# Float32 scores for the first 256 tokens only, in a hashed-attention and Mish feed-forward kernel

## The chip, the cores and the metric

The kernel runs on one core of one Trainium2 chip. The metric is the device time of one execution in microseconds (us): the median of several runs. A profile is one more execution, recorded instruction by instruction by the hardware profiler.

The engines are named as in the profile: PE is the matrix engine (PEld its weight loads), DVE the vector engine, ACT the scalar engine, POOL the GpSimd engine, and SP the queue from which all DMAs of this kernel are issued.

## The reference, cut to what matters

```python
# q, k, v: (4 batches, 8 heads, 768 tokens, 64), float32; proj: (64, 6)
q_bucket = sum((q @ proj > 0) * 2 ** arange(6));  k_bucket = the same of k
scores = where(q_bucket == k_bucket, q @ k.T / 8, -1e9)
attn   = exp(scores - max);  attn /= sum(attn) + 1e-9
x      = (attn @ v), heads side by side          # 3072 tokens x 512
h      = x @ w_in                                # 512 -> 2048
out    = (h * tanh(softplus(h))) @ w_out         # 2048 -> 512; w_in, w_out arrive as float64
```

## The kernel before, in words

The work is cut into **units** of 256 tokens: three units make one of the four batches, twelve units in all (u = 0 to 11). A unit has eight **slots** of attention, one for each of its two halves of 128 tokens and each of four pairs of heads (pair j = 0 to 3); slot n belongs to unit n // 8. A slot S computes 128 x 768 scores for both heads of its pair; then the row maxima (line 978, DVE), the factors of the softmax ("mb", lines 961 to 973), two exponentials (line 991, ACT), and the division with a split into two fp16 halves (lines 387 to 416) follow. The halves are transposed by DMA (line 472, tile PT) and multiplied with V (line 1088). In unit 0 alone the attention weights stay float32 and are transposed on PE (line 434), the product with V is float32 (line 1062), and so are its two feed-forward products (lines 1120 and 1169). The feed-forward part of a unit (H, Mish, O) runs three blocks of four slots behind its attention, and the sixteen pieces of the two float64 weights are converted on ACT, DVE and POOL during units 0 and 1 (lines 594 to 607, and w_hi and w_lo).

**Two ways to compute scores.** The usual way holds Q and K as two fp16 halves side by side in the contraction, and hash bits as six signs beside a second copy: a slot is eight fp16 matmuls (`pe` in att_front, line 937). To get there a block of keys or queries is squared and summed (line 480), scaled into a high half (k_hi, q_hi), copied (k_cp, q_cp), reduced to the low half (k_lo, q_lo), transposed by DMA, hashed by small matmuls (line 739), reduced (hsum, line 743), turned into bits (line 748) and transposed by DMA once more. The halves are laid out in the two buffers tok0 and tok1 before their transposes; units' queries and these keys share them, so one preparation follows the other.

The other way, `pe32` (line 948), takes raw float32 Q and K, transposed on PE (`turn32`, line 450, copied out at line 453), and bits from a float32 hash matmul (`hash32`, lines 461 and 464). It needs no fp16 preparation. F32U says how many units use it, and NF how many pairs: in the kernel before, F32U = 3 and NF = 2, so in units 0, 1 and 2 (the whole first batch) pairs 0 and 1 use float32 scores and pairs 2 and 3 the fp16 ones. The keys of these two pairs are transposed once, at the start (`k_prep32`); the queries of units 1 and 2 once for each unit (`q_prep32`), and their other eight heads go the fp16 way (`q_prep` from column 8 on, by `q_cuts`).

**The order.** The functions only list operations. ORDER, a table found offline, names them by number in the order in which they are issued to the engines; every engine takes its own in that order. A letter behind a number picks an alternative engine from the operation's list (none is the first of them).

Of the kernel before, what the change touches and what calls it, by code (L numbers as in the profile page):

```python
# [93 lines left out]
137 7 9 8 50 20 0 5 11 19 12 22 1 2 3 4 76 80 29 81b 13 37 6 77b 14 15 10 25 33 26 30b 38 17 27 28 18 34 39 52  # L94
60 61 35 62 41 56 54 63 57 55 21 42 48 51 53 24 23 31 78 36 32 64 65 16 86 91 138 92 79 87 147 40 88 82 117 83
43 118 44 119b 93 89 66 109 110 111 153 90 94 120 67 112 154b 132 107d 46 108 133 113 95 115 68 114 116 124
125b 155 121 126 101 84 45 134 136 135 156 127b 178 96 128 140b 148 141 47 58 149 85 122d 123 97 99 142 139b
98b 143 129 168d 179 180d 100 174 176 69 175 177 170 130 157 171b 131 172 173b 204 205b 169 70 145b 182 189
144b 102 158 159 181 161b 190b 71 193 291 194 195 185 191 150 186 192 220 221 103 222d 183b 187 206 160b 196
188 197 104 223 212 152 146 49 151 162 59 105 106 213b 207 216 218 217b 219b 214 215b 184 353 224 243 163 239  # L100
164 244 245b 241 248 240 242 233c 270 368 307 210d 208 235 254 236 255 249 209b 237 246 238 247 225 256 271
250 257 234 272d 262 263 268 266 292 198 273 226 267b 211 227 293 165 294 269 251 283 284 349 350 264 303 265
285 295 166 304b 354 305 296 258 199 200 309d 286b 310 311c 260c 261 306 274 281 313 253 252 232 228 282 312b
322 201 317 364 287 365 288 289 290 366 318 319 355b 323 324 308 320 321 367 330b 331 315 338 339 72 231 203
202 167 229 397 369b 314 329 316 325 297 298b 275 276b 340 333 341 230 332b 334 342 73 370d 299 336 425c 277
74 426 371 399 378 379 380 335 328 302 400 398 300 373 424 423 351 337 301 280 381 427 372b 374 382 389c 411
376 259 375 278 279 406 429 458 428 390 412 452 407 352 391 383 384b 393 392c 395 326 327 385 453 408d 409 410
415d 343 344c 356c 416 451 430 456 345 431 432 394 377 459 386 418 346 457 396 401 417b 454 433 387 348 347
413 419 455 75 357 434 443d 488b 460 421 444 461 420 388 422 441 404 435 436 414 402 445 489 490b 447 437 462d
463 464 478d 403 446c 449 479 405 465 438 466b 471 472b 487 523 518 493 494 495c 486 358 359 467 496 480b 482b  # L110
497 448 481b 484 360 491 510 525 532 511 442 450 361 512b 533 534 535 362 526 524 468 483 513b 492 439 546 514
474 536 552 485 469 470 537 519b 475c 476 516 473 520 538c 539 553 515 517 586 540b 521 554 440 477 498 499b
500 501 555d 542 522 541c 556 557 573b 574 575 548 549b 550 527 503 502 544 577 590 545 543 578 528 530 504
505b 591 592 547 588 506 594 593 507 576b 595d 587 581 612 603 604 551 582 583b 579 596 598c 529 559 558 531
589 597 613 599 580 363 618 600 560 561 562 614d 616 584b 615 632c 563 564c 601 566 651 508 509 585 633 647
634c 648 655 659 640 617 567 649 636 650 652 664 653 605 635 656 565 619 620 621 660 654 638 622 623c 625 568
569 602 639 661d 609 668 606 641 663 662 681b 682 683c 642 626 637 570b 691 607b 608 685 657 665 666 571b 627
# [12 lines left out]
964 952 962 965b 938 986 967 953 981 980 995c 974c 1029 1067 1031 983 987 1005 1004 996 997c 999b 975b 988  # L130
998b 1001b 1006 1007b 1009 1008 966 1066 1010 1011 1012b 990 1158 1021 870 886 1032 1192 1193 984b 993 991 992
994 1022 1023 1019 1003 1033 1069 1030 1194 1024 1000 1014 1025 1039d 1050 1002 1015 1223 1068 985 1013c 1040
1016b 1017 1051 1052d 1041c 1070 1071c 1053 1043 1054 1195 1055c 1042b 1034 1044 1073 1018 1082 1077 1020 1038
1196 989 1045 1083 1074 1086 1056 1057b 1059 1058c 1061b 1072b 1046 1060 1063 1078 1079c 1081 1080 1095c 1197
1064b 1096 1105 1106 1107c 1108 1097b 1098b 1198 1084 1099 1109 1087 1110b 1111 1062 1112 1101b 1036 1047
1085b 1090 1100 1102 1121 1122 1035 1123 1114 1124 1150 1154 1125 1075c 1076 1113b 1127c 1128 1116 1088b 1129b
1093 1155 1136 1137 1138 1104 1168 1119 1037 1115 1117 1139 1131 1140 1048 1091 1130c 1133 1141b 1142 1143b
1145 1151 1159 1089 1160 1132 1144 1161 1103 1164 1118 1120 1134 1146 1147 1162 1163 1152b 1199 1177d 1156
1178 1092 1200 1179b 1181b 1094 1187 1126 1065 1148 1172 1049 1201 1188 1189c 1165 1190 1191 1207c 1252 1182
1218 1180c 1183 1157 1184 1208 1209c 1153 1166 1211b 1224 1169 1175 1173 1225 1219 1220d 1221 1222 1174 1176  # L140
1210c 1213 1253 1212 1135 1149 1185 1170b 1236c 1237 1239 1238 1226 1228b 1214 1229 1186 1215 1247 1282 1202
1278 1216 1248 1249 1250 1203 1240 1251 1267c 1242 1167b 1268 1205b 1269c 1171 1271 1286 1287 1288b 1241 1283
1279 1230 1235 1243 1204b 1206 1280b 1295 1291 1284 1290 1289 1270c 1273 1285 1405 1308d 1281b 1309 1231 1310c
1272 1227 1254 1255 1274 1318 1256 1275 1257 1258c 1233b 1319 1232 1260 1320 1312 1311b 1314 1234 1299 1217
1292 1321 1322 1313 1338 1339 1340c 1304c 1349 1244 1350 1302 1300 1296 1401 1301 1351b 1342b 1261 1315 1293b
1276 1397 1341b 1305 1406 1297c 1353 1294 1303 1344 1352 1245 1355d 1356 1364 1317 1262 1316 1402 1259 1398
1418 1357c 1365 1324 1462 1343 1323 1345 1359 1263 1366 1367 1368 1265 1264b 1298b 1409 1360 1347 1388c 1389
1325 1326 1358b 1361 1399c 1327 1414 1346 1410 1411 1390 1391 1412 1392 1413 1394 1328 1306b 1307b 1403 1266
1329b 1431 1432 1400 1246 1362 1433c 1441 1442 1330c 1443 1393 1395 1331 1415 1419 1354 1348 1396 1435 1444
1434 1445 1370 1369 1332 1422 1457 1363 1425 1423 1416c 1437 1446d 1404 1447 1448b 1450b 1424 1426 1371 1372  # L150
1458 1459d 1333 1334 1336 1461 1460 1475c 1439 1373 1440 1454 1486 1502 1436 1438 1503 1374 1375 1335 1420
1384 1377 1449c 1476 1452 1451 1478c 1407 1487 1488b 1477b 1479b 1489 1490 1337 1506 1378 1379 1380 1453 1480
1515 1510 1421b 1376b 1504 1505b 1381b 1382b 1417 1481 1482 1491b 1507 1492 1493c 1495 1511 1494 1463 1464
1465c 1467 1408 1496 1512d 1383 1807 1516 1513 1514 1528d 1455 1456 1497 1529 1474 1385 1386 1519 1538 1520
1539 1540c 1499 1587 1517b 1530b 1532b 1541 1387 1468 1469 1483 1498 1542 1543c 1544 1545 1484 1470 1531b
1518b 1534 1591 1466c 1427c 1521 1522 1554 1641 1277 1500 1642 1523 1588 1547b 1555 1643 1556 1533 1535 1537
1536 1583 1508b 1557 1558 1509 1428 1584 1524 1569 1471b 1546b 1472b 1548 1473 1429c 1560b 1561 1570 1571c
# [62 lines left out]
F32U = 3  # L220
# [1125 lines left out]
```

## Time and profile before

| | |
|---|---|
| median of 3 runs | 817.49 us (816.95 to 817.76) |
| the profiled execution | 817.2 us, of which the profile's span is 815.4 us |
| busy time in the span | PE 798.2, ACT 624.9, DVE 602.9, POOL 426.9 us |
| first slots of units 0, 1, 2, 3 start at | 14.9, 56.0, 120.5, 198.4 us |

Busy time is the union of an engine's instructions; a wait inside the span is idle time. Views by stretch give the same for a window of the span. In the timeline, a line is a run of like instructions with its start and its duration; the difference between the starts of two neighbouring lines is the time that the first one took from the engine.

### The profile page before, as it was taken

What the parts mean: (1) busy time and instruction counts of PE and PEld (TensorE: products, weight loads), DVE (VectorE), ACT (ScalarE), POOL (GpSimd) and SP (SyncE); (2) the same over time, 40 slices, a digit from 0 to 9 for tenths busy, and PEclk for the clock granted to TensorE, in tenths of its full rate; (3) what the DMA queues carried; (4) which work ended last, traced back from release to release, by engine and by line L of the source; (5) the groups of instructions that cost most, each with busy time, mean ns of one, the idle gap of its engine ahead of it and who ended that gap; (6) DMA issues with size and microseconds to landing.
All of it is one profiled execution on the core that took longest, in us unless ns stands there. A gap on an engine that the chain in (4) does not pass through costs nothing.

```text
span 815.4 us, 17000 instructions
## 1 busy us (share of the span) xinstructions
PE 798.2 (98%) x6546; PEld 549.6 (67%) x6546; DVE 602.9 (74%) x1103; ACT 624.9 (77%) x976; POOL 426.9 (52%) x434
## 2 busy tenths in 40 slices
PE   8899999999999999999999999999999999999998
PEld 5556666666676776676666676667676676776674
DVE  5888999988898778887887767768877675566211
ACT  4889998888696769889679698989779785677211
POOL 3564446554356773733585564344646758845120
PEclk9999999999999999999999999999999999999999
DMA  7958998989999969989989959999989577466200
GB/s 253 219 174 221 240 246 196 191 156 206 217 160 182 203 116 181 170 158 216 185 172 155 195 117 151 197 213 192 167 140 169 107 139 145 81 124 133 50 27 27
DMA packets 395489, 134.29 MB, mean 165 GB/s; under 512 B 365456, under 2 KB 386448, under 8 KB 395408
## 3 DMA queue, kind: packets, MB, share of 16 engines
q1 hardware_dynamic: 395408, 133.21, 81.2%
q8 instruction: 51, 0.84, 0.4%
q14 instruction: 30, 0.25, 0.1%
HBM read 35.65 MB, written 6.29 MB: 51 GB/s over the span
## 4 chain that ended last, share of the span: by engine, by line
PE 47%; ACT 1%; DVE 1%; DMA 1%; issue 0%; POOL 0%; SPq 0%; ACTq 0%; DVEq 0%
PE ps_s L937 7%; PE ps_o L1179 6%; PE ps_o L1181 6%; PE ps_o L1180 6%; PE ps_acc L1130 5%; PE ps_t L1088 5%; PE ps_acc L1132 5%; PE ps_acc L1131 5%; ACT pb L991 1%; DVE svb L978 1%; DMA out_dram<-ffb 1%; PE ps_t L739 0%; ACT L1315 0%; DVE hl L408 0%; ACT tok L480 0%
## 5 line engine op out<-in xcount | busy, mean ns | idle before, releaser
L991 ACT ACTIVATE pb<-ps_s,svb 128x768 f32<-128x768 f32 x184 | 180.9, 987 | 87.4 <-DVE svb L968 36.7
L978 DVE TENSOR_REDUCE svb<-ps_s 128x2 f32<-128x1536 f32 x92 | 161.3, 1753 | 40.2 <-PE ps_s L937 33.7
L1130 PE MATMUL ps_acc<-X,wo 128*128 128x256 f16 x616 | 167.9, 273 | 0.3 <-ACT ffb L1151 0.3
L1132 PE MATMUL ps_acc<-X,wo 128*128 128x256 f16 x616 | 167.9, 273 | 0.0
L1131 PE MATMUL ps_acc<-X,wo 128*128 128x256 f16 x616 | 167.9, 273 | 0.0
L1315 ACT ACT_TABLE_LOAD x117 | 150.1, 1283 | 2.0
L408 DVE SCALAR_TENSOR_TENSOR hl<-pb,svb,hl 128x768 f16<-128x768 f32 x131 | 140.3, 1078 | 13.8 <-POOL hl L390 9.8
L1181 PE MATMUL ps_o<-wi,ffb 128*128 128x512 f16 x352 | 133.4, 379 | 0.0
L1180 PE MATMUL ps_o<-wi,ffb 128*128 128x512 f16 x352 | 133.4, 379 | 0.0
L1179 PE MATMUL ps_o<-wi,ffb 128*128 128x512 f16 x352 | 133.4, 379 | 0.0
L937 PE MATMUL ps_s<-KT,QT 128*128 128x512 f16 (+1 forms) x656 | 120.1, 326 | 2.1 <-ACT pb L991 1.8
L390 POOL TENSOR_SCALAR hl<-pb,svb 128x768 f16<-128x768 f32 x68 | 71.0, 1046 | 75.9 <-DVE svb L1021 28.8
L937 PEld LDWEIGHTS <-QT 128*128 128x128 f16 x672 | 64.2, 98 | 40.5 <-issue 8.3
L1088 PE MATMUL ps_t<-PT,VT 128*64 128x256 f16 x1584 | 90.7, 273 | 0.0
L1088 PEld LDWEIGHTS <-VT 128*64 128x64 f16 x1584 | 84.8, 110 | 8.1 <-issue 7.6
L1151 ACT ACTIVATE ffb<-ps_acc,smalls 128x512 f32<-128x512 f32 x88 | 58.5, 684 | 33.5 <-PE ps_acc L1132 32.0
L415 POOL TENSOR_TENSOR hl<-pb,hl 128x768 f16<-128x768 f32 x45 | 75.0, 1667 | 3.8
L414 POOL TENSOR_SCALAR pb<-pb,svb 128x768 f32<-128x768 f32 x45 | 44.4, 987 | 48.0 <-ACT hl L392 21.4
L1131 PEld LDWEIGHTS <-wo 128*128 128x128 f16 x616 | 60.2, 98 | 13.3 <-issue 1.5
L1130 PEld LDWEIGHTS <-wo 128*128 128x128 f16 x616 | 60.2, 98 | 12.6 <-issue 0.5
L1132 PEld LDWEIGHTS <-wo 128*128 128x128 f16 x616 | 60.2, 98 | 7.0
L1181 PEld LDWEIGHTS <-ffb 128*128 128x128 f16 x352 | 34.4, 98 | 41.6
(240 smaller groups left out, 1300.5 us busy)
## 6 DMA issues: line engine op xcount, KB each, us to landing
out_dram<-ffb SPq DMA_DIRECT2D x22, 256.0 KB, 2.7
stg<-in_v_dram SPq DMA_DIRECT2D x13, 384.0 KB, 4.0
stg<-in_k_dram SPq DMA_DIRECT2D x12, 384.0 KB, 4.0
wo<-in_q_dram SPq DMA_DIRECT2D x9, 512.0 KB, 4.9
stg<-in_moe_w_in_dram SPq DMA_DIRECT2D x8, 512.0 KB, 4.6
stg<-in_moe_w_out_dram SPq DMA_DIRECT2D x6, 512.0 KB, 4.6
PT<-hl SPq DMA_TRANSPOSE x176, 4.1
wo<-in_moe_w_out_dram SPq DMA_DIRECT2D x5, 512.0 KB, 4.7
```

What stands on the lines that cost most here:

```text
L408: return [("DVE", 215 + 1.035 * n, port(lambda: nc.vector.scalar_tensor_tensor(out=dst, in0=src, scalar=sc, in1=hi, op0=ALU.mult, op1=ALU. ...
L937: nc.tensor.matmul(ps[:, hh * S + c0 * P:hh * S + c1 * P], QTb[:, u % 2, sl, qi], KTb[:, j, sl, hh * NCH + c0:hh * NCH + c1].rearrange("p ...
L978: op("max", [("DVE", 1755, lambda: nc.vector.tensor_reduce(out=sv[:, 0], in_=ps.rearrange("p (h e) -> p h e", e=S), axis=AX.X, op=ALU.max, ...
L991: EXP[n, hh] = op("exp", [("ACT", 1075, lambda hh=hh, t=t: nc.scalar.activation(pb[:, t], HOMES[n][0][:, hh * S:(hh + 1) * S], AF.Exp, bia ...
L1088: nc.tensor.matmul(pv[hh * D:(hh + 1) * D, y * 256:(y + 1) * 256], vt[:, w, hh * NCH + c], pt[:, hh, a * NCH + c].rearrange("p s t -> p (s ...
L1130: nc.tensor.matmul(o, wh, X[:, 0, c], start=(c == 0), stop=False)
L1131: nc.tensor.matmul(o, wh, X[:, 1, c], start=False, stop=False)
L1132: nc.tensor.matmul(o, wl, X[:, 0, c], start=False, stop=(c == NCC - 1))
L1179: nc.tensor.matmul(PS[f"o{s}"], gh, wh, start=first, stop=False)
L1180: nc.tensor.matmul(PS[f"o{s}"], gh, wl, start=False, stop=False)
L1181: nc.tensor.matmul(PS[f"o{s}"], gl, wh, start=False, stop=last)
L1315: for fn in plan.ordered("exp", lambda x: nc.scalar.preload_act_table_set(sets[x])):
```

## The change

F32U becomes 1. Float32 scores remain in unit 0 (pairs 0 and 1). For units 1 and 2:

- the calls of `q_prep32` fall away, and `q_prep` (with the squares before it) takes all sixteen head-halves instead of eight;
- the eight slots of pairs 0 and 1 use `pe` instead of `pe32`;
- the keys of pairs 0 and 1 are converted to fp16 halves after all: `kv_stat` and `k_prep` are listed for pair 0 behind slot 4 and for pair 1 behind slot 6 (the offset is 4; it was 1, unused while F32U was 3). This is a square, a statistic, k_hi, k_cp, k_lo, a DMA transpose, 12 hash matmuls, hsum, two bits, a second DMA transpose, for each pair;
- unit 1 takes its pairs in the order 2, 3, 0, 1 (`turned`), and needs four small "sig" operations instead of one.

```diff
 ORDER = """
-137 7 9 8 50 20 0 5 11 19 12 22 1 2 3 4 76 80 29 81b 13 37 6 77b 14 15 10 25 33 26 30b 38 17 27 28 18 34 39 52
...
-F32U = 3
+F32U = 1
...
     for j in range(NF if F32U < NU else 0):
-        later(2 * j + 1, kv_stat, 0, j, True)
-        later(2 * j + 1, k_prep, 0, j)
+        later(2 * j + 4, kv_stat, 0, j, True)
+        later(2 * j + 4, k_prep, 0, j)
```

ORDER is replaced as a whole: 2655 numbers instead of 2636. Counting the operations as the code lists them, the new table can be read. What it says of the operations around the change:

| operation | place in the new order | engine |
|---|---|---|
| bits of unit 1's queries, 16 instead of 8 | hash matmuls between slots 6 and 7; bits before slot 8; their transpose next in the SP queue after two weight loads | DVE, POOL (before: both on DVE, behind slot 8) |
| keys of pair 0 | square between the exponentials of slots 4 and 5; k_hi and k_lo around the maxima of slots 6 and 7; hash matmuls behind slot 8 | ACT; DVE, DVE; k_cp and bits POOL |
| keys of pair 1 | square behind the exponentials of slot 8; k_hi, k_lo, k_cp around the maxima of slots 9 and 10; hash matmuls behind slot 12 | ACT; DVE, DVE, DVE; bits POOL |
| bits of unit 2's queries | hash matmuls before slot 15, their transpose before slot 16 | POOL |
| over the whole order: attention's high halves ("hi") | | ACT 64 (was 53), DVE 60 (55), POOL 52 (68) |
| over the whole order: "mb" | | DVE 65 (74), POOL 31 (22) |

More of the change, by code (lines that the diff above doesn't have):

```diff
@@ L209 @@
[L209 removed]
+12 20 52 11 22 19 50 54 57 56 21 51 55 23 9 8 7 91 60 5 0 6 10 1 29 61 2 33 3 30 62 13 14 15 25 26 37 34 63
+147 92 94b 17 31 27 35 32 38 28 36 64 86 76 39 41 148 40b 42 77 65 18 84 87 88b 16 80 81 138b 4 140b 137 78 82
+79 83 90 89 117 66 67 43 118 109 110b 95 53 68 69 48 141 44 139c 119 93b 45b 46 132 111 70 112b 71 149 96 97
+120 124 125 121 126 115 107d 127 133 98b 113 174 153 122b 72 114b 154 99b 216 128 155c 116b 129b 130 131b 134d
@@ new lines @@
+289 284 285 201 202 317 279b 303 326 304b 327b 305 328 294 301d 280d 208 318 319 281 332 306b 302 314 203b
+204b 333 329 256 236 307 257 340 258 335 338 308 209 309 310 341 259c 342 272 240 273 345 383 384 385 205 211
+239 346b 347 261 343 386 210 334b 336b 344 353c 331 354 355b 337 361 362 416 73 418 352 348 295 320 356 296
+351 339 363d 364 260c 321c 357 365 389d 297 359 322 388b 397 417 419 298 430 390 391c 398 312 399d 74 323 431b
+358 392c 262 325 299 360 300 443 237 470 393 238 349 350 432 400 401 408c 442 444 445 446b 366 324 402 372 395
@@ new lines @@
+425 263 409 264 426 410b 367b 394 460 412 447 373 368 403c 475 477 427d 266b 411 429 414 428 471b 404 265b
+434b 435 396 436b 374 472 448 449 476 450 451d 75 473c 478 405 369 506 413 437b 438 376 440 453 452 462d 371
+415 420 267 407 370 406 479 463 474 375 490 421 454 433 423 491b 484 507 455 464c 480 422 537 542 505 551 456
+457 466 492 485c 424 486 481d 482 483 497d 377 378 512 508 498 513 379 487 439 461 441 465b 509 489 488 467
+493 543 381b 380b 514d 494c 499 500b 510 468 495 544 458 511 565 605 566 545 538b 539 459 540c 501 541 517 496
@@ new lines @@
+1108b 1147 1136 1148b 1169 1173 1155 1156 1157 1123 1174 1122 1187 1170 1158 1150 1149c 1242 1151 1159 1112
+1152 1160c 1161 1162 1164 1178 1179 1180 1182 1181 1196c 1137 1138 1171 1163b 1166 1183 1145 1172 1111 1113
+1188 1175b 1197 1218c 1153 1165 1206 1207 1208b 1167 1220 1139 1191 1198 1184 1200 1199b 1176b 1209 1210 1226
+1227 1202 1243 1244 1237 1168 1154 1238 1201 1229c 1239 1203 1228 1192 1230b 1231 1245c 1247 1248 1271 1193
+1205 1204 1235 1241 1240 1194 1255d 1185c 1232b 1195 1256 1258c 1257 1266 1221 1186b 1267 1268c 1301 1297 1269
@@ new lines @@
+1259 1222 1223b 1261 1270 1224b 1424 1286b 1249 1305 1233 1287 1288c 1189c 1290b 1260 1262 1225 1298 1302 1234
+1314 1254 1310 1306 1307 1289c 1292 1190 1309 1308 1337 1250 1246c 1327 1328 1329c 1331 1273 1274 1291 1275
+1330c 1276 1236 1068 1293 1084 1299 1251b 1300b 1252 1333 1315 1311 1312b 1303b 1338 1339c 1313b 1277c 1340
+1341 1318 1263 1253 1481 1332 1304 1264b 1357b 1358 1359 1319 1325 1279 1334 1368 1369 1370c 1323b 1321 1324
+1360c 1320 1416 1294 1361b 1371 1278 1420 1322 1363 1372 1374c 1375 1376b 1316c 1342 1280 1362 1364 1343 1295
@@ new lines @@
+1383 1335 1281 1336 1378b 1379 1296 1384 1282 1385 1317 1421 1386 1387 1407c 1377c 1380 1326 1417 1344 1283
+1418 1389 1381 1365 1366 1428 1373 1367 1433 1345 1346 1415 1429 1430d 1437 1408 1410b 1413b 1409 1411 1412
+1431 1432 1434 1425 1419 1422c 1450d 1347 1284 1451 1348c 1453 1438 1452c 1426 1350 1454b 1460 1461 1462d 1464
+1463 1465 1382 1414 1441 1285 1265 1388 1351 1349 1442 1444 1390 1391 1443 1445 1466 1423b 1456b 1455 1457
+1476 1458 1352 1459 1435 1467b 1477 1353 1478 1469 1392 1521 1470 1479 1480 1468 1505 1393 1394c 1355 1436
@@ new lines @@
+1354 1356 1471b 1494b 1396 1495 1397 1497 1496 1506 1507b 1498 1508 1509 1510b 1395 1473 1525 1474 1526 1482
+1500 1511 1472 1529 1398 1475 1530 1399 1483 1512b 1403 1531 1514 1522 1439b 1484b 1532 1533 1547c 1486 1538
+1493 1534 1523 1501 1499 1513c 1440 1535 1548 1524 1516 1401b 1400b 1448 1549 1536 1551b 1557 1558 1515 1539
+1487 1402 1404 1518 1502 1405 1517 1660 1488 1606 1559c 1527 1550c 1519b 1560 1561 1485 1661 1489 1528 1427
+1701 1491 1562d 1540b 1573 1563 1553 1574 1575c 1490b 1564b 1566b 1577 1542 1492 1552 1406 1554 1556 1602 1571
@@ new lines @@
+1765 1786 1767 1789 1773 1774 1766 1793 1802 1753 1752 1775d 1776 1831 1777 1779b 1778 1768 1780 1794 1795b
+1787 1832b 1797 1796 1781 1834 1811b 1812 1813c 1815b 1799 1790b 1803 1821 1782 1835 1822 1823c 1825 1824
+1841b 1842 1843 1814b 1791 1817 1754 1760 1806 1852 1699 1816 1683 1818 1833c 1809 1807 1858 1845b 1846 1853
+1854d 1855 1856 1870c 1844 1859 1783 1860c 1808 1862 1847b 1871 1810 1873 1872 1800b 1769 1804 1863 1886 1848
+1820 1819 1881 1836 1850 1882 1883 1805b 1884 1874 1885 1901d 1876 1837 1839 1838 1902 1903c 1905 1801b 1916
@@ new lines @@
+1917 1849 1912 1920 1875 1840 1921 1904 1913 1864 1851 1869 1878 1909 1877 1906 1914 1922d 1861c 1865 1866b
+1924 1923 1888 1952 1907 1942 1918c 1889 1890 1891 1892b 1943 1867b 1915b 1925 1953 1945 1908 1933 1868 1894
+1954c 1955 1879b 1919 1948 1938c 1893c 1944b 1946b 1956 1972 1939 1973 1974b 1983 1895 1957 1947 2096 1949
+1958 1934 1910 1940b 1941 1935 2039 1926 1929 1950 1959 1975c 1930 1984 1985 1976b 1987 1986 1936 1989c 1978
+1927c 1937 1990 1991c 1993 1911 2031 2032 2035 1928b 1960 1931b 2036 1998 1896 1951 1897 1999 1961 2040 1899b
@@ new lines @@
+1898b 1962 1963c 2048 1981 1965 1932 2000d 2002 2001 2022d 2023 1979 2049 2024 2004 1977 2043 2044 1988 2041
+2045c 1992b 1995b 2033 1994 1900 2026 2046 1966 2003 2047 2065c 1980 2030 1967 1982 2052 2025c 2028 1964 2005
+2006 2066 2034 1968 1969 1970 1996 2027 1997 2007 2075 2037 2067b 2069 2038b 2008 2068b 2076 2077 2053 2054b
+2050 2009 2011 2055 2029 2056 2078 2079 2080c 2059 2074 1880 1971 2012 2010c 2071 2057 2091 2081 2058 2060
+2092 2051 2097 2098 2099c 2042 2089 2013 2070 2082b 2084b 2083 2014 2101 2093d 2072 2085 2140 2108 2086 2016b
@@ new lines @@
+2095 2094 2109c 2110 2111 2112b 2120 2121 2115 2122 2123 2102 2087 2073 2133 2136 2113 2018 2019 2020 2124
+2125d 2015b 2126 2127b 2144 2145 2146c 2129b 2141 2137 2148 2147 2088 2153 2090 2103 2116 2114 2017 2130 2275
+2100 2063c 2128c 2131 2132 2172 2061 2104 2162d 2106b 2163 2134b 2225 2173 2138b 2149 2117 2157 2165b 2164b
+2105 2166 2174 2176 2175 2139 2168 2064 2150 2177c 2142b 2118 2021 2158 2154 2188 2316 2178 2179c 2181 2189
+2155c 2276 2107 2169 2182 2167 2143b 2151 2152 2062 2315 2317 2190d 2191 2192 2194d 2195 2196c 2198 2277 2278
@@ new lines @@
+2180b 2199 2119 2217 2221 2170 2203 2204 2205 2185 2171 2222 2218 2235 2197 2160 2207 2183 2206 2208c 2226
+2184 2200 2209 2211c 2159 2214 2186 2187 2193 2231 2223 2210 2156b 2227 2228c 2212 2229 2230 2244b 2215 2201
+2213 2254 2202 2245 2161 2280 2232 2255 2256b 2257 2233b 2246c 2239 2216 2247c 2219c 2248 2258 2259d 2270 2220
+2252 2240 2241 2234 2250b 2224b 2253 2236 2242 2243 2322 2268 2271 2272 2273 2407 2237b 2135 2249 2281 2282
+2267 2260 2261c 2263 2274 2288b 2289 2262c 2265 2299 2251 2264 2290 2292 2300 2301 2302 2303 2291b 2294 2304d
@@ new lines @@
+2566 2519 2481 2314 2506 2483b 2492b 2509 2503 2567 2517b 2537 2527 2538 2539c 2504c 2505 2528b 2530b 2484
+2534 2520 2541 2500b 2570 2574 2507 2508 2540 2552 2535 2516 2518 2575 2529c 2568 2531 2543d 2544 2501 2532b
+2545c 2547b 2533 2548 2468 2536 2542 2553 2546c 2549 2554 2510 2571 2572c 2573b 2555 2556 2551 2565 2578 2576c
+2557b 2569 2579 2580b 2587 2588 2558 2560c 2563 2559 2561 2577 2581 2589 2590 2550 2564 2562 2591 2592 2582
+2593 2596 2585 2583 2584 2586 2594 2597 2599 2600 2601c 2602 2603 2615 2604 2607 2608 2609c 2605 2611 2616
@@ L210 @@
+2606 2617 2618 2610 2612 2613c 2614b 2627 2619 2620 2623 2624 2625b 2628 2626 2622 2631 2632 2633b 2634 2629c
+2630 2640 2635 2636 2621 2642 2639 2644 2641 2637 2638 2650 2595 2643 2645 2598 2651 2653b 2654 2652 2648b
+2646b 2649 2647
 """
```

165 lines of the change are left out of this document (50 added, 115 removed).

## The prediction

> **What bounds the kernel now.** I read the page's table of busy time first, then the same by stretch, then what PE waited for, then the timeline of PE around the slots that change.
>
> ```profile
> span 815.4 us, 17000 instructions
> PE 798.2 (98%) x6546; PEld 549.6 (67%) x6546; DVE 602.9 (74%) x1103; ACT 624.9 (77%) x976; POOL 426.9 (52%) x434
> ```
>
> PE is busy for all but 17.2 us. Over the whole span nothing else comes near. By stretch it looks different; the columns are the stretch, its length, then busy us and instructions of PE, PEld, DVE, ACT and POOL, the granted clock, the DMA share and GB/s:
>
> ```profile
> 15.00:56.00 41.00, 36.65 (x299) 23.68 (x299) 34.15 (x68) 32.38 (x67) 23.88 (x31) 1.00 0.82 208
> 56.00:153.00 97.00, 95.22 (x594) 62.89 (x594) 88.87 (x135) 88.90 (x141) 50.55 (x45) 1.00 0.94 216
> 153.00:210.00 57.00, 55.13 (x481) 38.82 (x481) 50.47 (x92) 48.70 (x73) 23.99 (x27) 1.00 0.93 186
> 210.00:760.00 550.00, 547.67 (x4683) 380.71 (x4680) 414.79 (x771) 439.68 (x671) 316.27 (x313) 1.00 0.86 162
> ```
>
> The first row is unit 0's attention: 4.35 us of PE idle in 41. The second holds the attention of units 1 and most of 2 with unit 0's feed-forward part and the weight conversion: PE idle 1.78 of 97 us, but DVE idle only 8.1 and ACT 8.1. After 210 us PE is the only engine near its limit (99.6%; DVE 75%, ACT 80%). So PE's own work sets the time, and in 56 to 153 two more engines stand 8% behind it. Of what PE waits for, 56 to 210 us, the longest (total, times, longest one):
>
> ```profile
> PE ps_s L937 <- ACT pb L991: 0.7, 2, 0.6
> PE ps_t L739 <- DVE hl L408: 0.7, 1, 0.7
> PE ps_t L1062 <- ACT PT L437: 0.6, 1, 0.6
> ```
>
> No DMA is among them, though the DMA share is 0.94.
>
> **The change, part by part.** PE's timeline (start, duration, line, what):
>
> ```profile
> 56.01 2.25 PE L948 MATMUL ps_s<-KT,QT 64*128 64x256 f32 x15
> ...
> 58.66 1.09 PE L450 MATMUL ps_t<-ffb,X 128*64 128x128 f32 x16
> 59.69 0.55 PE L434 MATMUL ps_l<-ffb,pb 128*128 128x128 f32 x3
> ...
> 71.61 2.25 PE L948 MATMUL ps_s<-KT,QT 64*128 64x256 f32 x15
> 73.79 0.18 PE L496 MATMUL ps_t<-smalls,ones 128*128 128x4 bf16 x1
> 73.83 0.16 PE L497 MATMUL ps_t<-floors,ones 128*128 128x4 bf16 x1
> 73.85 3.70 PE L1120 MATMUL ps_acc<-X,wi 128*128 128x256 f32 x16
> ...
> 86.78 1.02 PE L461 MATMUL ps_t<-QT,pw 128*128 128x512 f32 x2
> 87.84 1.46 PE L937 MATMUL ps_s<-KT,QT 128*128 128x512 f16 x8
> 89.14 1.88 PE L1169 MATMUL ps_o<-wo,ffb 128*128 128x512 f32 x4
> ```
>
> *Slots.* From start to next start a float32 slot takes 73.79 - 71.61 = 2.18 us, an fp16 slot 89.14 - 87.84 = 1.30. Eight slots change: 8 x 0.88 = 7.04 us of PE less. *Queries' float32 preparation.* A turn32 takes 59.69 - 58.66 = 1.03 us, a hash32 87.84 - 86.78 = 1.06; units 1 and 2 lose one of each: 4.18 us less. Removed: 11.2 us.
>
> *Added on PE.* A hash of eight query blocks:
>
> ```profile
> 47.66 0.35 PE L739 MATMUL ps_t<-pj,QT 128*128 128x12 f16 x8
> 47.87 0.53 PE L434 MATMUL ps_l<-ffb,pb 128*128 128x128 f32 x3
> ```
>
> 0.21 us for 8. The two key hashes have 12 each (0.32 x 2), the queries 8 more each (0.21 x 2), and the statistics are 73.85 - 73.79 = 0.06 each: 1.2 us. Net PE work: **-10.0 us**, of which turn32 and hash32 of unit 1 (2.1 us, at 22 to 28 us) lie in unit 0's stretch, and about -8 us in 56 to 153.
>
> *Added elsewhere.* Rows for one operation (line, engine, shapes, count, busy, mean ns, then idle before):
>
> ```profile
> L480 ACT ACTIVATE tok<-stg 128x768 bf16<-128x768 f32 x25 | 21.0, 841 | 5.4 <-DMA KT<-tok 2.0 <-DMA stg<-in_k_dram 1.9 <-DMA stg<-in_v_dram 1.1
> L748 POOL TENSOR_SCALAR tok<-hsum 128x72 f16<-128x72 f32 (+1 forms) x22 | 14.0, 641 | 15.2 <-DVE hsum L743 15.1
> L408 DVE SCALAR_TENSOR_TENSOR tok<-stg,smalls,tok 128x768 f16<-128x768 f32 x12 | 13.1, 1092 | 3.0 <-POOL tok L390 2.9
> L743 DVE TENSOR_REDUCE hsum<-ps_t 128x72 f32<-128x144 f32 (+2 forms) x26 | 8.1, 311 | 2.9 <-PE ps_t L739 2.2 <-POOL wo L748 0.4
> L399 POOL TENSOR_SCALAR tok<-tok 128x768 f16<-128x768 f16 (+1 forms) x4 | 3.5, 885 | 1.3 <-DMA KT<-tok 1.3
> L393 DVE TENSOR_SCALAR tok<-stg,smalls 128x768 f16<-128x768 f32 x5 | 3.1, 619 | 0.3
> L464 DVE TENSOR_SCALAR QT<-ps_t,smalls 128x512 bf16<-128x512 f32 x2 | 1.5, 743 | 0.0
> ```
>
> For each key pair the new order puts k_hi, k_lo and hsum on DVE: 0.62 + 1.09 + 0.31 = 2.0 us, with the short operations of the statistic some 2.4. Two pairs make 4.8. ACT gets two squares of at least 0.84. POOL gets four bits, 2.6 us, and a copy of 0.9. Queries of twice the width add at most one more such set between the engines, of which I count 0.5 us to DVE. Away go two hash32 results on DVE, 1.5 us, one of them in 56 to 153. The DVE bill in 56 to 153 is thus +4.8 + 0.5 - 0.7 = **+4.6 us**; three further sigs are below 1 us and lie beside matmuls. ACT gets +1.7 or a little more; POOL, idle for 46 us of the 97, can take its share.
>
> *What that does to PE.* If PE's idle time stayed as it is, 97 us would become 89. DVE would have 88.9 + 4.6 = 93.5 us of work in them. It doesn't fit, unless 4.5 us slide behind 153 us, where DVE has 57 - 50.5 = 6.5 us free before 210. Over 56 to 210, PE wants 154 - 8 = 146 us, and DVE has 139.3 + 4.6 = 143.9 of work: it fits at 98.6%, and what fits so tightly waits. Lower bound of the cost: 0, all slides. Upper bound: DVE's idle of 8.1 us in 56 to 153 stays and its 4.6 come on top, which eats the whole 8 and 4.6 more. I take **+2.0**: the new order also moves nine "mb" from DVE to POOL, and PE's idle in the old 56 to 210, with DVE at 90%, is 3.7 us, so a half more of that at 98% is near the lower end.
>
> [...]
>
> *Unit 0's stretch.* Its 2.1 us of PE lie among waits on ACT and DVE (4.35 us idle). Bounds: all kept, none kept; I take half, a loss of **+1.0**. The two copies of turn32's result that also go help neither bound.
>
> *DMA.* Four key transposes are new and the four query transposes of units 1 and 2 have twice the columns, all on the SP queue, ahead of weight loads and of transposes of PT. Bounds: nothing, as today no PE wait names a DMA; or a late one, below. I take 0. The cover is that PT is needed only three slots later and weights one block later.
>
> *Order.* The rest of ORDER is new too. After 210 us I see no cause for a change: PE idles 2.3 us in 550, so there is no gain left, and DVE and ACT have a fifth of the time free. I take 0, and a spread of 1 us each way.
>
> Sum on the profiled execution's own 817.2 us: -10.0 + 2.0 + 1.0 = -7.0, thus 810.2. The median of the runs is 0.3 above it: **810.5 us**.
>
> **The rivals.**
>
> *Full gain* (0.20): DVE's work slides without a stall, and the 1.0 is kept too: 817.5 - 10.0 = 807.5, 805 to 808 with the spread. For it: 6.5 us of DVE free behind 153, POOL half idle. Against: DVE must then run at 98%.
>
> *The gain dies in 56 to 153* (0.14): DVE fills its whole idle time and nothing slides: 97 becomes 93.5, and waits between DVE, ACT and PE cost some more: 814 to 818. For it: the rows of 92%; against: weight pieces' low halves are needed only in unit 1's feed-forward part, so they can slide.
>
> *DVE keeps its gaps* (0.07), the slower side: DVE's idle is waiting for scores, and its 4.6 us come on top: 817.5 - 1.1 + 4.6 = 821. It decides when less than 3.5 of the 8.1 us of gaps are filled. [...] Against: maxima wait for PE, and PE's scores come sooner now.
>
> *The fp16 queries come late* (0.09), slower too. Until now unit 1's fp16 queries had to be there only for slot 12 at 87.84; from now on slot 8 needs them.
>
> ```profile
> 59.96 0.18 DVE L748 TENSOR_SCALAR tok<-hsum 128x48 f16<-128x48 f32 x1
> ...
> 67.35 1.25 SPq L472 DMA_TRANSPOSE QT<-tok  x1
> ...
> QT<-tok SPq DMA_TRANSPOSE x24, 4.8
> ```
>
> The hash was done at 47.9, the bits began at 59.96 and their transpose was issued at 67.35; 4.8 us later it landed: 72.2. Slot 8 began at 56.01. Kept so, it costs 16.1 us: 817.5 - 10.0 + 16.1 = 824. It decides when that transpose is issued after 56.0 - 2 - 4.8 + 7 = 56 us. Against: the new order puts bits and transpose ahead of slot 8. The same holds for unit 2 and slot 16, where pair 1's keys must first leave tok0 and tok1; a wait of 1 or 2 us there is in my range.
>
> **How the numbers follow.** The forecast with its own range, 808 to 813.5, has 0.50; the rivals have 0.20, 0.14, 0.07 and 0.09. A measurement of this kernel tells 0.2% (1.6 us) from no change. Faster than 815.9: 0.50 + 0.20 + half of the dying gain = 0.77. Within 815.9 to 819.1: 0.09, from the other half with the milder late waits. Slower: 0.14. The range from 805.5 to 817 leaves out the two slower rivals and a little at each end.
>
> **What would show it.** PE busy falls by about 10 us (to 788) if the PE terms are right. Line 948 keeps 60 of its 180 matmuls. PE's idle time grows from 17.2 to about 20 us, most of it between unit 1's first slot and unit 3's, with DVE or ACT as releaser. Slot 24 starts at about 191 instead of 198.4. Wrong would be: a PE wait on a QT or KT transpose over 2 us before slots 8, 12 or 16 (queries or keys late); slot 24 at 196 or later (the gain died); PE idle above 22 us after 210 (the order).

## The result, and the profile after

The changed kernel takes **828.0 us** (median of 4 runs, 823.7 to 830.75) against 817.6 (816.95 to 818.5) of the kernel before on the same chip: ratio **1.012**, 95% interval 1.0097 to 1.0143. It is 10 us slower; 810.5 with a range of 805.5 to 817 had been forecast. The profiled run of it took 830.75, its span is 828.9. A second measurement later gave 826.9 (826.0 to 831.3), its profile a span of 824.2; where the two profiles differ, both are given.

The first lines of the page:

```profile
span 828.9 us, 16919 instructions
PE 796.5 (96%) x6498; PEld 547.3 (66%) x6498; DVE 623.4 (75%) x1122; ACT 614.2 (74%) x964; POOL 395.4 (48%) x415
```

PE is idle for 32.4 us, before for 17.2: that is 15.2 of the 13.5 us by which the span grew, and PE's busy time gives back 1.7 where 10.0 had been forecast. By stretch (columns as in the prediction):

```profile
15.00:56.00 41.00, 34.08 (x264) 21.59 (x264) 27.51 (x66) 29.47 (x56) 17.84 (x25) 0.88 0.87 197
56.00:153.00 97.00, 90.05 (x564) 60.24 (x566) 89.49 (x135) 90.31 (x143) 54.42 (x54) 1.00 1.02 230
210.00:400.00 190.00, 184.38 (x1596) 128.59 (x1594) 150.69 (x278) 157.15 (x243) 102.68 (x103) 1.00 0.94 175
```

Three things are new. In unit 0's stretch the granted clock is 0.88 (0.96 in the second profile) instead of 1.00. In 56 to 153 us PE stands idle for 6.95 us (6.4 in the second) instead of 1.78, while DVE and ACT are hardly busier than before (89.5 and 90.3 of 97, before 88.9 and 88.9). And in 210 to 400 us, where the operations are those of before, PE is idle for 5.6 us (3.9 in the second) instead of 1.9.

A fourth stands in the first lines of the page: DVE is busy for 20.5 us more than before, ACT for 10.7 less and POOL for 31.5 less. The added preparation is the smaller part of this, since without it (the run at 829.0 below) DVE is still busy for 619.7 us. The new order also gives operations to other engines, behind 210 us too (in 210 to 760 us DVE 14.1 more, ACT 15.9 and POOL 35.3 less).

What PE waited for over the whole span (total, times, longest):

```profile
PE ps_s L938 <- ACT pb L992: 7.9, 11, 1.9
PE ps_s L451 <- DMA wi<-in_k_dram: 2.7, 1, 2.7
PE ps_s L938 <- DMA KT<-wo: 2.3, 1, 2.3
```

The first row is a score bank that ACT's exponentials have not yet read. The second is a single wait for a load of keys before slot 0, which starts on time all the same. The third is a single wait in unit 0's stretch. From PE's timeline:

```profile
36.02 0.38 PE L938 MATMUL ps_s<-KT,QT 128*128 128x512 f16 x1
38.75 2.29 PE L938 MATMUL ps_s<-KT,QT 128*128 128x512 f16 x7 [2.34 <-DMA KT<-wo]
```

That is slot 4. The transpose of pair 2's bits that it waits for stands behind three loads on the SP queue, two of weights and one of queries (start, duration of the issue):

```profile
27.24 0.57 SPq L469 DMA_DIRECT2D wi<-in_moe_w_in_dram  x1
27.86 0.47 SPq L469 DMA_DIRECT2D stg<-in_moe_w_in_dram  x1
28.38 0.47 SPq L469 DMA_DIRECT2D X<-in_q_dram  x1
29.29 4.75 SPq L473 DMA_TRANSPOSE KT<-wo  x1
```

Its issue took 4.75 us, and the other seven matmuls of slot 4 could start 9.5 us after the issue began. In the kernel before, this queue reads:

```profile
31.98 1.76 SPq L472 DMA_TRANSPOSE KT<-wo  x1
```

From the end of this wait on the matmuls run at half the clock (windows of 4 us; the clock is the third column from the end). The first profile of the changed kernel, then its second:

```profile
40.00:44.00 4.00, 3.43 (x17) 1.86 (x16) 1.86 (x2) 0.48 (x1) 0.00 (x0) 0.50 1.08 248
44.00:48.00 4.00, 4.00 (x15) 2.16 (x15) 1.05 (x6) 1.82 (x3) 0.00 (x0) 0.50 0.65 190
```

```profile
40.00:44.00 4.00, 3.43 (x20) 1.86 (x19) 1.80 (x2) 0.70 (x2) 0.00 (x0) 0.77 1.12 251
44.00:48.00 4.00, 4.00 (x34) 2.51 (x32) 3.11 (x8) 3.84 (x7) 0.19 (x1) 1.00 0.71 201
```

PE looks full in the second row of the first profile, and it ran 15 matmuls where it ran 34 in the second one: a busy share without its clock misleads. The length of this phase differs from run to run, which is a part of the spread of the changed kernel's times: over its span the fastest run, 823.7, had a mean granted clock of 1.000, the slowest, 830.75, one of 0.994.

To follow the delay along the span, here is where slots start, each taken as the start of its maximum on DVE (us, and the difference to before):

| slot | before | after, first profile | after, second profile |
|---|---|---|---|
| 0 | 17.18 | +0.0 | +0.3 |
| 4 | 38.53 | +4.0 | +4.0 |
| 5 | 40.67 | +7.5 | +5.3 |
| 8 | 58.29 | +7.8 | +5.3 |
| 12 | 89.63 | +9.8 | +7.1 |
| 24 | 199.86 | +8.9 | +5.5 |
| 30 | 243.59 | +11.4 | +8.0 |
| 95 | 746.32 | +13.6 | +8.9 |

So 5 to 8 us are lost before slot 8. From slot 8 to slot 24, where 6 us were to be won, the time is that of before (141.57 before, 142.6 and 141.8 after). Behind slot 24, 3.4 to 4.7 more are lost.

### The profile page after: what moved, and what is told of

Its sections match the earlier page's. It is cut to its first block, busy times and chain, and to the rows that moved or that the text cites. A ratio compares the mean times of both kernels' runs of the same rounds, so it can differ in the third digit from the quotient of the medians.

```text
span 828.9 us, 16919 instructions
## 1 busy us (share of the span) xinstructions
PE 796.5 (96%) x6498; PEld 547.3 (66%) x6498; DVE 623.4 (75%) x1122; ACT 614.2 (74%) x964; POOL 395.4 (48%) x415
## 5 line engine op out<-in xcount | busy, mean ns | idle before, releaser
L938 PE MATMUL ps_s<-KT,QT 128*128 128x512 f16 (+1 forms) x720 | 133.1, 328 | 11.0 <-ACT pb L992 7.9
L938 PEld LDWEIGHTS <-QT 128*128 128x128 f16 x736 | 70.9, 98 | 54.2 <-issue 19.8
L391 POOL TENSOR_SCALAR hl<-pb,svb 128x768 f16<-128x768 f32 x52 | 56.8, 1093 | 97.1 <-DVE svb L1022 53.7
L416 POOL TENSOR_TENSOR hl<-pb,hl 128x768 f16<-128x768 f32 x43 | 73.0, 1697 | 3.6
L393 ACT ACTIVATE hl<-pb,svb 128x768 f16<-128x768 f32 x64 | 58.9, 929 | 14.7 <-DVE svb L1022 6.3
```

What stands on the lines that cost most here:

```text
L938: nc.tensor.matmul(ps[:, hh * S + c0 * P:hh * S + c1 * P], QTb[:, u % 2, sl, qi], KTb[:, j, sl, hh * NCH + c0:hh * NCH + c1].rearrange("p ...
```

## The experiments

Each was compared with the kernel before on the same chip, whose median was 816.9 to 817.2 throughout. "New order" is the ORDER of the changed kernel, "old order" that of the kernel before. Line numbers shift by up to six between kernels; the fp16 slot is the line with ps_s<-KT,QT at L932, L933 or L938.

**Which part costs it? The change on the old order, and the work of before in the new one.** Both by rule: an operation that both kernels have keeps its place in the order used, the others are put at the place, counted between slots, that they have in the other order.

```
F32U = 1   with the old ORDER, the changed operations put in   (first run)
F32U = 3   with the new ORDER, the old operations put in       (second run)
```

> The change (F32U = 1) issued in the order of the kernel before: every operation that both kernels have keeps its old place and engine, and only the new ones (key conversion of pairs 0 and 1, three sigs, unit 2's query preparation) take the place they have in the new order. Theory A (the loss is the new order's first 60 us, where PE starves and its granted clock falls): no half clock, slot 8 is reduced at 56 to 60 us instead of 66, and the time is 812 to 820 us. Theory B (the loss is the fp16 preparation itself, wherever it stands): still 825 to 830 us.

> The kernel before (F32U = 3, float32 scores in three units, no key conversion) issued in the new order. Theory A: slot 4 late again, granted clock near 0.5 for some us, slot 8 reduced at 64 to 67 us, 824 to 832 us. Theory B: within 2 us of the kernel before, 816 to 820 us, since the preparation is gone.

Measured: 866.0 (ratio 1.060) and 847.2 (1.039). Neither tells of the change: the placement made waits of its own (11.6 us of a hash matmul for DVE in the first; a turn waiting 7.8 us for a load in the second). Three later attempts to place them better fared no better:

```
F32U = 3 in the new ORDER, transposes of unit 1 behind slot 0
F32U = 1 in the old ORDER, key conversion and wide queries put in afresh
F32U = 1, old ORDER up to slot 8, new ORDER behind
```

> A second try at the kernel before in the new order: operations that only the kernel before has are placed by their place between the slots (the first try put unit 1's transposes on PE before slot 0, where they waited for a load that came 13 us late). Theory A: 824 to 832 us with a starved PE before slot 8. Theory C: 816 to 822 us.

> A second try at the change in the order of the kernel before; the new operations and the query preparations of units 1 and 2 are placed by their place between the slots. Theory A (the order of unit 0 costs 8 us, the rest is DVE and ACT): slot 8 reduced at 57 to 61 us, total 815 to 821 us. Theory D (no order found by moving a few operations holds, the plan is tight everywhere): over 828 us.

> The changed kernel with unit 0 (up to slot 8) in the order of the kernel before and everything behind it in the new order. Theory A: no clock drop, slot 8 at 57 to 61 us, and the rest as in the changed kernel: 818 to 823 us. Theory D: over 828 us.

Measured: 861.9 (1.056), 849.5 (1.040), 842.0 (1.031). In the last two, hash matmuls waited 4.3 and 5.1 us for the transpose of unit 1's queries, which fp16 slots from slot 8 on need early. These five show how much a misplaced operation costs here, and not what the change costs. The slot 8 of the first of these three, 8.3 us late without any of the added preparation, can't be laid to the new order alone either: its slot 2 is already 6.1 us late, where that of the changed kernel is 2.5 late.

**The fp16 slots alone, in the old order.** The eight float32 slots of units 1 and 2 run as fp16 slots on the keys of pairs 2 and 3 and the queries of unit 0, which are there; nothing else is touched.

```
-                qi = (2 * j + hh) * 2 + s
+                y, z = (0, j + 2) if f32 else (u % 2, j)
+                qi = (2 * z + hh) * 2 + s
...
-        op(f"S{n}", [("PE", 1900, pe32) if f32 else ("PE", 1290, pe)], ...
+        op(f"S{n}", [("PE", 1900, pe32) if f32 and u < 1 else ("PE", 1290, pe)], ...
```

> The kernel before with the eight float32 slots of units 1 and 2 run as fp16 slots, on the fp16 keys of pairs 2 and 3 and unit 0's buffer of queries (so these slots compute other scores); nothing else is added or removed. PE's work falls by 7.0 us. If PE's work sets the time in 56 to 153 us: 810 to 812 us. If DVE and ACT set the pace there (the rival rule): 814 to 818 us.

Measured: 814.65, ratio 0.9976 (0.9961 to 0.9991): 2.6 us of the 7.0 that the slots were to save. PE's busy time fell by 5.7 us and the span by 2.9; the difference is PE idle time, most of it between 60 and 210 us. First the row of before, then that of this run:

```profile
60.00:210.00 150.00, 146.43 (x1039) 98.94 (x1038) 135.58 (x224) 134.13 (x206) 71.45 (x68) 1.00 0.95 207
```

```profile
60.00:210.00 150.00, 143.97 (x1017) 97.43 (x1016) 138.26 (x226) 136.89 (x212) 75.63 (x70) 1.00 0.95 214
```

PE's idle time goes from 3.57 to 6.03 us; DVE and ACT rise to 92 and 91%; in no kernel of this study did either get above 92.2% here.

**The late transpose and the clock.** In the first run the three loads go behind the transpose of pair 2's bits. In the second, small matmuls that nobody reads are put in before slots 4, 6 and 7 to keep the clock up.

```
-  ... 47 58 24 49 100 59 ...
+  ... 47 100 58 24 49 59 ...
```

```
+    hold(ps_s, 40); hold(ps_s, 12); hold(ps_b, 24)   # before slots 4, 6 and 7
```

> The changed kernel with one move in the SP queue: the transpose of pair 2's key bits is issued ahead of the three loads of 512 KB that stood directly before it. Theory A (this transpose landed behind those loads, PE waited 2.3 us and its clock fell): slot 4 starts 2 to 4 us earlier, the granted clock stays at 1.0 in 38 to 48 us, 820 to 824 us. Theory B: no change, 826 to 830 us.

> The changed kernel with idle matmuls on ones (40 before slot 4, 12 before slot 6, 24 before slot 7; 4.2 us of PE at full clock) into the bank that the slot overwrites, so that PE is not idle while slot 4 waits. If the fall of the granted clock costs what the profiled execution shows (busy time of the same matmuls in unit 0 is 4 us longer): clock 1.0 from 38 to 48 us, slot 8 at 62 to 64 us, total 823 to 826 us with a smaller spread than 823.7 to 830.8. If the clock is a by-product only: 828 to 832 us.

Measured: 827.3 (825.9 to 828.2, ratio 1.0128) and 829.4 (1.0155). With the transpose first, slot 4 starts on time (+0.0), but slot 7 is late by 6.3 and slot 8 by 4.3 us all the same, and the end by 10.3. With the held clock:

```profile
44.00:48.00 4.00, 3.88 (x39) 2.60 (x36) 3.54 (x5) 3.53 (x7) 0.49 (x2) 1.00 0.69 196
```

The clock is whole until 52 us (0.60 in 52 to 56 us), and slot 8 is still 6.8 us late. Taking away the late transpose or the early fall of the clock leaves the time within 2.5 us of the changed kernel's 826.9 and 828.0. For the transpose that says that it is not the main loss. For the clock it says less, since the 76 added matmuls take PE's time themselves (4.2 us as estimated before the run; in 36 to 40 us PE is busy for 3.73 us and not 1.66): what the clock alone costs is not shown, and the changed kernel's run at a mean clock of 1.000 is still 6 us slower than before.

**The added preparation.** The changed kernel in its new order without the key conversion of pairs 0 and 1; with queries of half the width in units 1 and 2; without both. Pairs 0 and 1 of units 1 and 2 then read the keys or queries of pairs 2 and 3 instead. The squares and statistics of the two key pairs (`kv_stat`) stay in all three.

```
-        later(2 * j + 4, k_prep, 0, j)                                   (first, third)
-        return [(4 * NF, 16)] if u < F32U else [(0, 16)]                 (second, third)
+        return [(4 * NF, 16)] if u < NU else [(0, 16)]
```

> The changed kernel without the key conversion of pairs 0 and 1 (their k_prep is left out, 18 operations of which four are DMA transposes; the slots that need these keys read those of pairs 2 and 3, so they compute other scores). Order otherwise as in the changed kernel. Theory C (in the first 200 us DVE, ACT and the DMA queue set the pace with PE, so each added preparation costs about its DVE time, 2.4 us a pair, and more where PE starves): 818 to 823 us. Theory A (only the order and the late transpose before slot 4): 825 to 829 us, as that transpose is untouched.

> The changed kernel with the fp16 query preparation of units 1 and 2 at its old width of eight head-halves (the slots of pairs 0 and 1 read the queries of pairs 2 and 3, so they compute other scores). Theory C: about 2 us less than the changed kernel, 823 to 827 us. Theory A: no change within 1 us.

> The changed kernel with both left out, key conversion and the wider queries. What is left is PE's saving of 11 us and the new order. Theory C: 812 to 818 us, like the kernel before with fp16 slots (814.65). Theory A: 822 us or more, since the new order's first 60 us stay.

Measured: 828.3 (1.0136), 828.9 (1.0153) and 829.0 (1.0147, 1.0132 to 1.0162). In the new order leaving the preparation out wins nothing that would stand out of the spread of these kernels, some 2 us each way. The changed kernel once more, beside these:

> The changed kernel once more, as the reference for the three above on the same chip: 824 to 831 us. In a profile whose granted clock stays at 1.0, slot 8 is reduced 3 to 5 us earlier than at 66.1.

Measured: 826.9 (826.0 to 831.3), ratio 1.014 (1.011 to 1.017). Its profile is the second one above: the clock did fall, but for a shorter time, and the maximum of slot 8 starts at 63.5 us, 2.6 us earlier than in the first.

**The parts of the change one after the other, in the old order without deadlines.** The fp16 slots on other keys as above; first without the float32 queries of units 1 and 2, then with the key conversion too, then with the wide queries too. No slot reads what is added, but the added preparation shares the buffers tok0 and tok1 with that of the queries.

```
-        if u < F32U:
-            later(q_at, q_prep32, u)                                     (all three)
+    for j in range(NF):                                                  (second, third)
+        later(2 * j + 4, kv_stat, 0, j, True)
+        later(2 * j + 4, k_prep, 0, j)
-        return [(4 * NF, 16)] if u < F32U else [(0, 16)]                 (third)
+        return [(4 * NF, 16)] if u < 1 else [(0, 16)]
```

> The kernel before in its own ORDER. The scores of pairs 0 and 1 of units 1 and 2 run as fp16 slots on the keys of pairs 2 and 3 and the queries of unit 0 (they are not those of the reference), and the float32 queries of units 1 and 2 are not prepared. PE's work falls by 7.0 + 4.2 = 11.2 us and DVE's by 1.5; nothing of the added preparation is there. It does about the work of the changed kernel without its added preparation, which took 829.0 in the new order. Theory 'the order': 812 to 814 (the eight slots alone gained 2.6 of 7.0; 4.2 more at the same rate are 1.5), 15 us below the new order. Theory 'the fp16 slots can't be used': about 817, no gain; the new order is then guilty of 12. If PE alone set the time: 806.

> The kernel of the run before with the conversion of the keys of pairs 0 and 1 added (statistic, hi, lo, copy, hash, bits, four transposes), placed in the old ORDER without a deadline, since no slot reads what it makes. DVE gets up to 4.8 us, ACT 1.7, POOL 3.5, PE 0.8, the SP queue four transposes. Theory 'the order': DVE and ACT have the room, 0 to 1.5 us above the run before. Theory 'DVE pays' (its gaps in 56 to 153 us stay, the added work comes on top): 4 to 5 us above it, 817 to 819.

> As the run before, with the fp16 queries of units 1 and 2 prepared at twice the width, as in the changed kernel, in the old ORDER. Now all the work of the changed kernel is there, and only the deadlines are not: the fp16 slots of pairs 0 and 1 read other keys and queries. Theory 'the order': 813 to 816, 12 or more below the changed kernel; what the change lost is then the order that its deadlines led to. Theory 'DVE pays': 818 to 822.

Measured: 817.07 (814.2 to 819.1, ratio 0.9998, 0.9986 to 1.0010), 828.1 (1.0139) and 830.4 (1.0164). The first comes out as the second theory has it, the other two miss both. The first has, by the sum, 11.2 us less work on PE and 1.5 less on DVE than before, nothing added, and gains nothing, not even what the slots alone had gained:

```profile
60.00:210.00 150.00, 141.69 (x982) 95.91 (x984) 136.70 (x221) 134.65 (x207) 73.69 (x69) 0.99 0.95 206
```

A part of this is the clock. In this profile it is 0.59 in 24 to 28 us and 0.79 in 60 to 68 us, shortly behind the places where the float32 queries had been transposed on PE; with the slots alone, where that work is still there, it is 1.00 in both. Over 15 to 60 us it is 0.96 in this run and in the three built on it, 1.00 before and with the slots alone. PE's busy time fell by 5.8 us only, as with the slots alone. Of the ten runs the two with a mean clock of 1.000 took 814.2 and 815.9 us. So at a mean clock of 1.000 the 11.2 us bring about what the slots alone bring, 1 to 3 us, and in the median of the ten nothing.

The second, with the keys' conversion added to it, is as slow as the changed kernel. Its row:

```profile
60.00:210.00 150.00, 136.91 (x951) 92.88 (x950) 135.43 (x217) 133.40 (x206) 69.39 (x71) 0.99 0.92 205
```

With about 5 us of added work on DVE (its busy time over the span rises by 5.3) the kernel is 11 us slower, and DVE, ACT and PE are all *less* busy in this stretch than without the addition. The timelines show two places where the time goes (slot 7's, then three lines of slot 11's):

```profile
52.69 0.55 PE L429 MATMUL ps_t<-ffb,pb 128*128 128x128 f32 x3 [2.99 <-DVE smalls L496]
77.79 1.03 POOL L394 TENSOR_SCALAR tok<-tok 128x768 f16<-128x768 f16 x1 [7.38 <-DMA QT<-tok]
78.85 0.84 ACT L475 ACTIVATE tok<-wi 128x768 bf16<-128x768 f32 x1 [3.17 <-POOL tok L394]
88.31 2.25 PE L933 MATMUL ps_s<-KT,QT 128*128 128x512 f16 x7 [2.12 <-ACT pb L988]
```

In the first, a transpose on PE waits 3.0 us until DVE, which has the maximum of slot 6 and its factors to do before, has read a statistic; everything behind it on PE is held up (+0.9 at slot 6, +3.1 at 7, +4.2 at 8). The second begins with a DMA: POOL's copy of pair 0's keys waits 7.4 us for the transpose of query bits out of the shared buffers, ACT's square for pair 1 waits for that copy, and the exponentials stand behind that square on ACT, so that PE waits 2.1 us for its score bank (+4.2 at slot 10, +8.1 at 11, +9.8 at 12, then +9.5 at the end). So the 11 us are waits at two places and not 5 us of DVE work, and they belong to this placement as well as to the work; another placement was not tried. My theory that the new order is the whole loss is not borne out: the same 11 us appear in the old order when the key conversion is put into it by this rule.

**What paces 60 to 210 us, if not PE?** The first of these three, with the low halves of PT in slots 12 to 23 computed over half the columns.

```
-            op("lo", ...(hlb[:, y, 1], pb[:, t], rv, hlb[:, y, 0], S)
+            op("lo", ...(hlb[:, y, 1, 0:S // 2], pb[:, t, 0:S // 2], rv, hlb[:, y, 0, 0:S // 2], S // 2)   # 12 <= n < 24
```

> The kernel before in its own ORDER with fp16 slots on other keys and queries and without float32 queries of units 1 and 2 (PE 11 us less, 817.07, no gain), and the low halves of PT in slots 12 to 23 computed over half the columns: 24 operations of 1.1 us become 0.55, some 13 us less on DVE between slots 12 and 24, about 8 of them in 56 to 153. Theory 'DVE and ACT pace 56 to 153 and PE does not': slots 12 to 24 shorten by 3 to 8 us, 809 to 814. Theory 'a fixed chain of waits paces it, no engine': no gain, 816 to 817. Theory 'PE's work sets it': no gain either, and PE without waits, which its 6.4 us of idle time already speak against.

Measured: 815.65 (814.4 to 817.7), ratio 0.9986 (0.9975 to 0.9997): 1.4 us below the run that it is built on, whose interval overlaps this one. From slot 12 to slot 24 it took 110.1 us, without the shortening 110.5.

```profile
60.00:210.00 150.00, 141.71 (x1008) 96.54 (x1010) 130.32 (x224) 135.03 (x208) 64.11 (x69) 1.00 0.98 208
```

DVE has 6.4 us less to do in this stretch than in the run it is built on and POOL, which does some of the low halves, 9.6 less; PE is no busier, ACT stands at 90% as it did. DVE by itself does not pace the stretch either. ACT is the one of the four whose work was not shortened; the largest of PE's waits on one line in 60 to 210 us names ACT in several kernels (before 0.7 us in all, fp16 slots alone 2.2, changed kernel 3.0). Whether shorter exponentials would help was not tried.

**The end.** The changed kernel with the old order behind slot 24, where both have the same operations; and the same with the three loads behind the transpose.

```
 ORDER: new up to slot 24, behind it the 1,876 common operations in the old sequence
-  ... 47 58 24 49 100 59 ...                                             (second)
+  ... 47 100 58 24 49 59 ...
```

> The changed kernel whole, its new ORDER up to slot 24 and the order of the kernel before behind it (1,876 operations, units 3 to 11, whose work the change does not touch). In the new order the stretch from slot 24 to slot 95 took 2 to 5 us longer than before in every kernel that had it, in the old order -0.8 to +1.5. Theory 'the order behind 210 us costs by itself': 3 to 5 us below the changed kernel, 823 to 824.5, and slot 95 no further behind than slot 24. Theory 'the end is late because the front ends in another state': as the changed kernel, 827 to 828.

> As the run before, with the three weight loads issued behind pair 2's transpose of bits on the SP queue, as in the run that did this alone (slot 4 on time, slot 24 5.2 us late instead of 8.9). Theory 'two losses of the order, independent of each other': 821 to 823. If the tail makes up for what the front gains or loses: 827.

Measured: 826.1 (825.5 to 827.05, ratio 1.0114) and 824.3 (823.7 to 824.8, ratio 1.0091). With the old order, slots 24 to 95 lose 0.8 us instead of 3.4 to 4.7, but slot 24 itself came 3.3 later at the joint; the net is 1 to 2 us, less than the 3 to 5 expected. The transpose in time gives another 1.75 here. Together: the best version of the change that was run, still 7.4 us slower than before.

## Why the prediction was wrong

*PE's work.* The terms were nearly right. Of line 949's matmuls 60 are left, as said. PE's busy time fell by 1.7 and 4.9 us (two profiles) and not by 10.0, but it was counted at a lower clock: 0.89 and 0.96 in 15 to 60 us, worth at most 5.0 and 1.8 us of 45. By this estimate it fell by up to 6.7 in both. The slots' term is too large: by themselves they took 5.7 us off PE's busy time, not 7.04. The rest of the 3.3 is not assigned.

*The step that failed is the one from PE's work to time: "about -8 us in 56 to 153", less "+2.0" for DVE.* It took PE's saved work for saved time and set the price by adding up DVE's work: "it fits at 98.6%". No kernel came near this. In 60 to 210 us DVE reached 92.2% at most and ACT 91.7%, and each engine's idle time was no room: as the two waits above show (3.0 and 2.1 us of PE), an engine that works off a fixed order stands still with work left behind the one operation that waits. From slot 8 to slot 24 the gain forecast was 8 less 2.0; it was -0.3 and -1.1, and 3.4 with the slots alone. And PE's work was worth little there to begin with: 7.0 us less gave 2.6, 11.2 us less gave nothing (1 to 3 us at a mean clock of 1.000). That the clock would be lower with PE's work removed (0.96 in 15 to 60 us in the four runs in the old order without the float32 queries, 1.00 before) was not in the sum. "PE's own work sets the time" was read from a PE that was busy for 98% of the time, and it is true only as long as PE has this much to do: others stood right behind. In this stretch the outcome was that of the rival "the gain dies in 56 to 153", at 0.14; its reason, DVE's filled idle time, did not hold, since 6.4 us less on DVE didn't bring the gain back. The time of the whole, 828, lies above every rival's, 824 at most: this step explains the gain that is missing, and the loss beside it arose in two places to which the prediction gave +1.0 and 0.

*The order, taken at 0, is the largest miss.* Without the key conversion and with queries of half the width the kernel takes 829.0 in the new order and 817.07 in the old one. The operations are nearly the same (the new order's run keeps the squares and statistics of two key pairs), so that most of 12 us belong to the order: its sequence, and the engines that it chooses, which put DVE at 619.7 us and not 602.7. The bill of +4.6 for DVE counted the added operations alone, though the table of the change shows operations moved off POOL.

*Unit 0's stretch, "+1.0", was mis-sized:* slot 8 should have been 1.1 us early and was 5.3 to 7.8 late, 6.4 to 8.9 us off. It is not mainly the preparation, without which slot 8 is 6.9 us late. The sum counted the work that leaves the stretch and not what the new order does to the rest of it: keys transposed on PE between slots 0 and 1 instead of before slot 0 (slot 1 is 2.5 us late), another sequence of loads, the late transpose, the clock behind it. How the 5 to 8 us divide among these is not shown.

*"DMA: I take 0"* failed at one place. "PT is needed only three slots later and weights one block later" covered those transposes, but pair 2's bits have no such cover, and three loads moved ahead of them. In time, they give 1.75 us with the old order behind slot 24 (824.3 against 826.1), and nothing clear in the new order (827.3 against 826.9 and 828.0).

*"After 210 us: 0"* was wrong by 3.4 to 4.7 us. The order alone does it, as its replacement shows; the net worth of it is 1 to 2. PE's idle time in 210 to 760 us is 8.0 us (5.6 in the second profile), not 2.3, and the threshold named, 22 us, was set so high that it could not have shown it.

*Queries or keys late before slots 8, 12, 16:* did not happen. No wait of PE on a QT or KT transpose over 2 us lies there, and half-width queries change nothing (828.9). Slot 16 is 17.7 and 14.8 us late, some 6 more than slot 15, without such a wait: the new order puts more of PE's other work before it, and by slot 20 the delay is down to 10.0 and 6.9. The sign for a gain that dies did come: slot 24 starts on PE at 205.9 and 202.5 us, "at 196 or later".

*What stays open.* With the preparation the kernel takes 827 to 830 in either order; without it the old order takes 817 and the new one 829. Why the new order loses its 5 to 8 us before slot 8 is only known in part, and what sets the pace from 60 to 210 us is not shown: of the single engines PE and DVE are ruled out, ACT is not. An order written for the changed work and as well matched to the chip as the old one is to its own might do better; none was found here, and these runs can't say how good it would be. By the old order with nothing added (814.65 with the slots alone, 817.07), there is little to be won even then.

## What to carry to other kernels

Where every engine works off a fixed sequence, an engine that is 98% busy is a bound only until it gets a few us less to do; then look at what stands 8% behind it, and price the gain by a run that takes the work away and adds nothing (here 2.6 us of 7.0, and 0 of 11.2). Read the granted clock of that run too: here it was 0.96 and not 1.00 in 15 to 60 us with the float32 queries left out. Don't fill another engine's idle time in a sum: where 5 us of DVE work went in between operations of a DVE that was idle for 14 of 150 us, the kernel lost 11 us: one late operation stopped all that stood behind it on PE for 3.0 us, and a shared buffer carried a wait of 7.4 us on POOL to ACT (3.2 us) and PE (2.1 us). And when a change replaces the whole sequence, price the new sequence as part of the change, also where it touches little or nothing else: here 9 to 12.5 us were lost before slot 8 and behind slot 24.

## What the runs showed of the hardware

The granted clock of the changed kernel fell to 0.50 from 38 us on. In the first profile it is 1.00 in 36 to 38 us, 0.53 in 38 to 39, 0.50 in 39 to 48, 0.70 in 48 to 48.5 and 1.00 in 48.5 to 54; in the second 1.00 in 36 to 38, 0.62 in 38 to 40, 0.53 in 40 to 42 and 1.00 in 42 to 48. In 36 to 38 us, ahead of the fall, PE was busy for 0.40 us (0.63 in the second profile), in the kernel before, whose clock stayed at 1.00, for 1.54. The longest single wait of the changed kernel's PE around the fall was 2.34 us. With the matmuls added before slot 4, PE was busy for 3.73 of the 4 us from 36 to 40, and the clock stayed at 1.00 until 52 us. What brings the fall about and what sets its length is not shown.

A DMA transpose issued behind three loads took 4.75 us to issue (1.76 before, with one load ahead of it; 1.28 in the run that put it ahead of the loads), and SP's next issue came only at its end, at 34.08 us. How many loads stand ahead does not decide it alone: the changed kernel's next transpose, with one load ahead of it, took 4.34 us, and the one after that, again with one load ahead, 1.45.
